# Two attention stages and a gated feed-forward layer: in batches 3 and 4 all six groups of stage 1 share one maximum and one sum

## The chip, the cores and the metric

The kernel runs on one NeuronCore of one Trainium2 chip. The metric is the device time of one execution, in microseconds (µs). Before the change three runs gave a median of 714.13 µs (713.99 to 714.23).

The engines are named as the profile names them: PE is TensorE (matrix products; PEld its weight loads), DVE is VectorE, ACT is ScalarE, POOL is GpSimd, and SP is SyncE, which here only starts DMAs. Each engine works through its own list of instructions in order and waits for others by semaphores.

## The reference, cut to what matters

```python
def mab(q, kv):                                   # one attention
    s = scale * (q @ kv.transpose(0, 2, 1))
    s = s - s.max(-1, keepdims=True)
    a = np.exp(s)
    a /= a.sum(-1, keepdims=True) + 1e-09
    return a @ kv
h = mab(I, x)                                     # stage 1: 32 inducing points attend to 12416 tokens
y = mab(x, h)                                     # stage 2: every token attends to the 32 rows of h
gate = 1.0 / (1.0 + np.exp(-(y @ w_gate)))        # feed-forward, 128 -> 1536 -> 128
out = (gate * (y @ w_val)) @ w_out
```

There are 4 batches of 12416 tokens with 128 channels. Stage 1 needs a maximum and a sum over all tokens of a batch, and stage 2 of a batch can only begin when stage 1 of that batch is complete.

## The kernel before

**Tiling.** A batch has 97 columns of 128 tokens: six groups of 16 columns (numbers 0 to 5) and one column left over (number 6, `NG` in the code). Stages 1 and 2 work by groups, the feed-forward by blocks of four columns (512 tokens).

**The main loop.** A block passes through the feed-forward in 8 steps, by turns of two and of one 128-wide slices of the 1536. `product(t)` issues for step t the matmuls that fill `v_ps` (the value half), the fill of the gate half `g_ps` for step t + 2, and the VectorE instruction that multiplies both halves into `u` (L1071). `gate(t + 2)` is ScalarE's tanh (L1053), which reads `g_ps` into `t`. `project` multiplies `u` by the output weights (L1106), and ScalarE copies the finished block out (L1124). For a two-slice step the product `u` of step t is made to wait for the gate fill of step t + 2, which itself waits until tanh of step t has emptied the same PSUM bank. So tanh, gate fill and product follow one another.

**Slots.** Two steps make a slot. All other work is placed by hand: `at(slot, make)` puts an instruction behind the first step of that slot, and `late=True` behind the second. The loop calls these as it passes; nothing is reordered later. With o = 96 the slots counted from o are those in which batch 2 goes through the feed-forward and stage 1 of batch 3 is computed beside it; with o = 192 the same for batches 3 and 4. In the trace slot 0 of these is at about 201 µs (o = 96) and 369 µs (o = 192), and a slot takes about 1.75 µs.

**Stage 1 beside the loop** (`plan_stage1` and `plan_shared`). The scores of one group fill one PSUM bank, tag `m`, of which there is one; all work beside the loop takes it in turn. In batches 3 and 4 there were two ways for a group before the change:

- Groups 2 and 3, each on its own (`plan_stage1`): VectorE takes the maximum straight from PSUM (L248), ScalarE the exponential from PSUM (L261), the tile is transposed by DMA, the sums are accumulated and copied out by ScalarE (`s1_sum_keep`, L311).
- Groups 0, 1, 4 and 5 together (`plan_shared`): ScalarE copies the scores to SBUF (`keep`, L358), into parts of the transposed input `xT` that nobody reads any more. GpSimd raises one common maximum elementwise, one group after the other (`lift`, three instructions L375, L376 and L379), halves it to 128 columns and joins the left-over column. VectorE reduces those 128 columns (`low`, L389). GpSimd subtracts the maximum from the scores (`lower`, L403), ScalarE takes the exponentials (`weigh`, L407), and pairs of groups share one accumulation in PSUM (`PER` = 2), each copied out once (`hold`, L421).

`plan_combine` then weighs the partial results (two own and two shared, `NSH` = 4) by their maxima and adds them on GpSimd (`least`, `join`).

**Stage 2 beside the loop** (`plan_stage2`). ScalarE copies scores to SBUF (`keep`, L636), GpSimd subtracts each token's maximum (`s2_lower_pool`, L646 to L653), ScalarE takes the exponential (L662), GpSimd adds up (`total`, L670), inverts (L453 to L458) and multiplies (`spread`, L692, tile `a2n`), and a DMA transposes the result for the main loop. GpSimd does the work of both stages in the order of the slots.

Of the kernel before, what the change touches and what calls it, by code (L numbers as in the profile page):

```python
# [9 lines left out]
F32 = mybir.dt.float32  # L10
F16 = mybir.dt.float16
# [6 lines left out]
P = 128  # L18
GC = 16
# [7 lines left out]
def kernel(  # L27
# [10 lines left out]
    B, N, C = x.shape  # L38
    m = inducing.shape[0]
# [4 lines left out]
    NG = NCH // GC  # L44
    NLO = NCH - NG * GC
# [12 lines left out]
    s2p = ctx.enter_context(tc.tile_pool(name="s2p", bufs=2))  # L58
    up = ctx.enter_context(tc.tile_pool(name="up", bufs=6))
    tp = ctx.enter_context(tc.tile_pool(name="tp", bufs=4))  # L60
    op = ctx.enter_context(tc.tile_pool(name="op", bufs=3))

# [114 lines left out]
    arrival = [0, NG] + list(range(1, NG))  # L179
    at_col = {s: p for p, s in enumerate(arrival)}  # L180
    EARLY = NS - 3
    SHARED = [(), (0, 1)] + [(0, 1, 4, 5)] * (B - 2)
    own = [[s for s in (arrival if b == 0 else [2, 3, 4, 5]) if s not in SHARED[b]] for b in range(B)]
    col_of = [{s: p for p, s in enumerate(o)} for o in own]
    PER = [1, 1] + [2] * (B - 2)
    NSH = [len(own[b]) + len(SHARED[b]) // PER[b] for b in range(B)]
    nml = const.tile([P, 1 + NS - EARLY], F32, tag="nml")
    l1l = const.tile([P, 1 + NS - EARLY], F32, tag="l1l")
# [24 lines left out]
    def at(slot, make, late=False):  # L213
        plan.setdefault((slot, late), []).append(make)
# [130 lines left out]
    def plan_shared(b, o, takes, tops, least, weighs, sums, holds, one, with_one):  # L345
        st = {}
        nm, hst, ns, no = nm1s[b % 2], hsts[b % 2], NSH[b], len(own[b])
        per = PER[b]

        def place(i):  # L350
            c = NLO + 8 * i
            return xT[b - 1][:, c : c + 8, :].rearrange("p j t -> p (j t)").bitcast(F32)

        def score(i):
            st["s1"] = s1_score_pe(b, SHARED[b][i], "m")

        def keep(i):
            nc.scalar.copy(out=place(i), in_=st["s1"][:])  # L358

        def score_one():  # L360
            s1 = s1_score_pe(b, NG, "m")
            st["one"] = s1p.tile([P, 512], F16, tag="a1T", name="one").bitcast(F32)[0:m, 0:P]
            nc.scalar.copy(out=st["one"], in_=s1[0:m, 0:P])

        def weigh_one():
            st["a1T"] = s1p.tile([P, 512], F16, tag="a1T", name="a1T")
            nc.scalar.activation(out=st["a1T"][0:m, 0:P], in_=st["one"], func=AF.Exp)

        def turn_one():
            st["a1"] = s1p.tile([P, 4, P], F16, tag="a1", name="a1")  # L370
            nc.sync.dma_start(st["a1"][:, 0, 0:m], st["a1T"][0:m, 0:P], transpose=True)

        def rise(near, far, w, R=P):
            top, r = place(4)[0:R, 0:w], place(5)[0:R, 0:w]
            nc.gpsimd.tensor_tensor(out=r, in0=far, in1=near, op=ALU.subtract)  # L375
            nc.gpsimd.tensor_scalar(  # L376
                out=r, in0=r, scalar1=BIG, scalar2=0.0, op0=ALU.min, op1=ALU.max
            )
            nc.gpsimd.tensor_tensor(out=top, in0=near, in1=r, op=ALU.add)  # L379

        def lift(i):
            rise(place(0) if i == 1 else place(4), place(i), 512)
            if i == len(SHARED[b]) - 1:
                for w in (256, 128):
                    rise(place(4)[:, 0:w], place(4)[:, w : 2 * w], w)
                rise(place(4)[0:m, 0:P], st["one"], P, m)

        def low():
            nc.vector.tensor_reduce(  # L389
                out=nm[:, no : no + 1],  # L390
                in_=place(4)[:, 0:128],
                axis=AX.X,
                op=ALU.max,
                negate=True,
            )
            lower(place(0), st["one"], place(1))
            for k in range(no + 1, ns):
                nc.gpsimd.tensor_copy(out=nm[:, k : k + 1], in_=nm[:, no : no + 1])

        def lower(*parts):  # L400
            for far in parts:
                near = nm[0 : far.shape[0], no : no + 1].to_broadcast(far.shape)
                nc.gpsimd.tensor_tensor(out=far, in0=far, in1=near, op=ALU.add)  # L403

        def weigh(i):
            st["a1T"] = s1p.tile([P, 512], F16, tag="a1T", name="a1T")
            nc.scalar.activation(out=st["a1T"][:], in_=place(i), func=AF.Exp)  # L407

        def turn(i):
            st[i] = s1_turn_dma(b, SHARED[b][i], st["a1T"])  # L410

        def part(i, k0, k1):
            if i % per == 0 and k0 == 0:
                st["hp"] = ps.tile([P, C + 1], F32, tag="m", name="hp_ps")
            if i == with_one and k0:
                s1_sum_pe(b, NG, st["a1"], st["hp"], 0, 1, False, False)
            s1_sum_pe(b, SHARED[b][i], st[i], st["hp"], k0, k1, i % per == 0, (i + 1) % per == 0)

        def hold(k):
            summed[b] += 1  # L420
            nc.scalar.copy(out=hst[:, no + k, :], in_=st["hp"][:])  # L421

        for i in range(len(SHARED[b])):
            at(o + takes[i], lambda i=i: score(i))
            at(o + takes[i], lambda i=i: keep(i), late=True)
            at(o + weighs[i], lambda i=i: weigh(i), late=True)
            at(o + weighs[i] + 1, lambda i=i: turn(i))
            at(o + sums[i], lambda i=i: part(i, 0, 2))
            at(o + sums[i] + 1, lambda i=i: part(i, 2, 4))
        at(o + one[0], score_one)  # L430
        at(o + one[1], weigh_one)
        at(o + one[1] + 1, turn_one)
        for i, slot in enumerate(tops):
            at(o + slot, lambda i=i: lift(i + 1))
        at(o + least, low)
        if len(SHARED[b]) > 2:
            at(o + least + 6, lambda: lower(*[place(i) for i in range(2, len(SHARED[b]))]))
        for k, slot in enumerate(holds):
            at(o + slot, lambda k=k: hold(k))
# [68 lines left out]
    def plan_combine(b, lead, weights, joined, taken, fill):  # L508
# [5 lines left out]
        def least():  # L514
            ml = bp.tile([P, 1], F32, tag="ml")
            src = nm1[:, 0:1]
            for k in range(1, ns, 2):
                nc.gpsimd.tensor_scalar(
                    out=ml[:],
                    in0=src,  # L520
                    scalar1=nm1[:, k : k + 1],
                    scalar2=nm1[:, min(k + 1, ns - 1) : min(k + 1, ns - 1) + 1],
                    op0=ALU.min,
                    op1=ALU.min,
                )
                src = ml[:]
            st["col"] = join_min(bp, ml)

        def weigh():
            st["w"] = bp.tile([P, NS], F32, tag="w1", name="w1")  # L530
# [65 lines left out]


    a2 = {}

    def s2_score(b, c, j0, j1, s2, whole=False):  # L600
        for j in range(j0, j1):
# [109 lines left out]
    def plan_stage2(b, c, score, take, weigh, far=None, soon=False, lag=None, low=None):  # L711
# [58 lines left out]
        if soon:  # L770
            for k in range(2):
                at(weigh - 1 + k, lambda k=k: s2_shift(GC, st["s2"], *st["hl"], which=(k,)))
        else:
            at(take, keep, late=True)
            at(low or take if lag is None else lag, lower, late=lag is None)
        at(weigh, exp, late=True)
        at(weigh + 1, total)
# [279 lines left out]
    def product(t):  # L1057
        st = steps[t]
        hidden_mm(st, "v")
        if t == 0:  # L1060
            keep_on(3, "acc")
        if t < T0:
            gate_fill(t + 2)
        else:
            single_fill(2 * (t - T0) + 3)
            single_fill(2 * (t - T0) + 4)
            st["t"] = ring_t(2 * (t - T0), 2)
        st["u"] = up.tile([P, st["cnt"], 512], F16, tag=f"u{st['cnt']}", name="u16")
        cuts = [0, 256, 512] if t == 0 else [0, 512] if t < NST - 1 else [0, 384, 512]
        for c, e in zip(cuts, cuts[1:]):  # L1070
            u = nc.vector.scalar_tensor_tensor(  # L1071
                out=st["u"][:, :, c:e],
                in0=st["t"][:, :, c:e],
                scalar=1.0,
                in1=st["v"][:, :, c:e],
                op0=ALU.add,
                op1=ALU.mult,
            )
            if t == 0 and c == 0:
                turn_b()  # L1080
        if st["cnt"] == 2 and 4 <= t < T0:

            tc.declare_no_dep(u.ins, st["tanh"].ins, reason="the gate fill of t + 2 waits for it")
            tc.add_manual_dep(
                u.ins, gates[t + 2]["gend"].ins.name, AFTER, reason="tanh, gate fill, product"
            )
# [46 lines left out]
    for b in range(B):  # L1133
# [30 lines left out]
            turns = (5, 7, 17, 19, 22, 25, 9)  # L1164
            shared = (10, 14), (15,), 20, (26, 30), (33, 42), (34, 43), (13, 25), 0
        else:
            parts = {2: (7, (16, 17, 17)), 3: (11, (18, 19, 19))}
            turns = (-14, -5, -3, 2, 0, 8)
            shared = (
                (-6, 2, 10, 14),  # L1170
                (7, 11, 15),
                23,
                (26, 30, 42, 46),
                (40, 42, 49, 51),
                (45, 53),
                (9, 27),
                3,
            )
        plan_shared(b + 1, o, *shared)
        for s, (score, total) in parts.items():  # L1180
# [90 lines left out]
```

## Time and profile before

| | before |
|---|---|
| time, median of 3 runs | 714.13 µs |
| span of the profiled execution, first to last instruction | 712.4 µs |
| around the span (difference of the two) | 1.7 µs |
| PE, ACT busy in the span | 649.5 µs (91%), 678.6 µs (95%) |
| POOL busy in the span | 449.2 µs (63%) |
| granted TensorE clock | 0.998 of full speed |

The profiled execution has no time of its own beside its span; the 1.7 µs come from the median of the runs. Busy time is the time in which an engine has an instruction under way. Successive instructions of one engine overlap a little in the records, so the step from one start to the next is shorter than a recorded duration. In a row of the timeline stand the start in µs, the time that the row covers, engine, line, operation, `output<-inputs`, shapes and the number of instructions merged into it; in square brackets the engine's idle time before it and what ended it.

### The profile page before, as it was taken

What the parts mean: (1) busy time and instruction counts of PE and PEld (TensorE: products, weight loads), DVE (VectorE), ACT (ScalarE), POOL (GpSimd) and SP (SyncE); (2) the same over time, 40 slices, a digit from 0 to 9 for tenths busy, and PEclk for the clock granted to TensorE, in tenths of its full rate; (3) what the DMA queues carried; (4) which work ended last, traced back from release to release, by engine and by line L of the source; (5) the groups of instructions that cost most, each with busy time, mean ns of one, the idle gap of its engine ahead of it and who ended that gap; (6) DMA issues with size and microseconds to landing.
All of it is one profiled execution on the core that took longest, in us unless ns stands there. A gap on an engine that the chain in (4) does not pass through costs nothing.

```text
span 712.4 us, 21620 instructions
## 1 busy us (share of the span) xinstructions
PE 649.5 (91%) x8475; PEld 394.2 (55%) x8475; DVE 694.2 (97%) x806; ACT 678.6 (95%) x1103; POOL 449.2 (63%) x785
## 2 busy tenths in 40 slices
PE   7999899998999999999998989999899999899996
PEld 4555455555555555655555655555555555555555
DVE  4799999999999999999999999999999999999997
ACT  4799999999999999999999999999999999999996
POOL 4568865877558978668657887587748356372300
PEclk9999999999999999999999999999999999999999
DMA  8979964263693174155485142221222131221201
GB/s 171 176 136 174 149 129 103 76 120 81 118 159 81 57 126 103 56 120 114 92 149 112 53 76 67 55 76 38 70 76 61 46 60 60 61 61 46 71 37 46
DMA packets 117110, 65.23 MB, mean 92 GB/s; under 512 B 100208, under 2 KB 101392, under 8 KB 117008
## 3 DMA queue, kind: packets, MB, share of 16 engines
q1 hardware_dynamic: 112320, 49.83, 31.4%
q0 software_dynamic: 4416, 13.90, 11.1%
q8 instruction: 66, 1.08, 0.6%
q14 instruction: 36, 0.29, 0.1%
q10 hardware_dynamic: 272, 0.13, 0.1%
HBM read 27.80 MB, written 25.43 MB: 75 GB/s over the span
## 4 chain that ended last, share of the span: by engine, by line
DVE 38%; PE 30%; issue 15%; ACT 14%; DMA 2%; DVEq 1%; POOL 0%; ACTq 0%; POOLq 0%
DVE u L1071 36%; PE acc_ps L1106 14%; PE v_ps L1022 11%; ACT t L1053 11%; PE g_ps L1022 2%; DMA xn<-in_x_dram 2%; ACT o L1124 2%; ACT xn L1045 1%; PE hp_ps L296 1%; DVE nm L248 1%; DVEq L1071 0%; POOL xn L95 0%; ACT a1T L261 0%; ACT e L662 0%; ACT hwt L483 0%
## 5 line engine op out<-in xcount | busy, mean ns | idle before, releaser
L1071 DVE SCALAR_TENSOR_TENSOR u<-t,v_ps 128x512 f16<-128x512 f16 x609 | 528.8, 947 | 1.0 <-ACT t L1053 0.5
L1053 ACT ACTIVATE t<-g_ps 128x512 f16<-128x512 f32 x609 | 464.5, 821 | 11.0 <-ACT t L1053 4.3
L1106 PE MATMUL acc_ps<-wo,u 128*128 128x128 f16 x4656 | 334.5, 220 | 3.2 <-ACT o L1124 0.8
L1106 PEld LDWEIGHTS <-u 128*128 128x128 f16 x4656 | 262.7, 98 | 112.9 <-issue 109.4
L1022 PE MATMUL v_ps<-a2r,hwt 32*128 32x512 f16 (+1 forms) x1188 | 278.6, 372 | 47.1 <-DVE u L1071 43.5
L1022 PE MATMUL g_ps<-a2r,hwt 32*128 32x512 f16 (+1 forms) x1188 | 293.6, 376 | 0.5 <-DVE u L1071 0.2
L1022 PEld LDWEIGHTS <-hwt 32*128 32x128 f16 x2424 | 92.0, 91 | 156.7 <-issue 104.3
L1071 DVE SCALAR_TENSOR_TENSOR u<-xn,v_ps 128x1024 f16<-128x1024 f16 (+1 forms) x127 | 142.9, 1206 | 0.3 <-PE g_ps L1022 0.3
L1045 ACT ACTIVATE xn<-g_ps 128x512 f16<-128x512 f32 x249 | 129.0, 606 | 1.9 <-PE g_ps L1022 0.6
L692 POOL TENSOR_TENSOR a2n<-e,rs 128x2048 f16<-128x2048 f16 (+3 forms) x25 | 86.8, 3475 | 5.0 <-DVE rs L681 2.1
L670 POOL TENSOR_TENSOR sum<-e 128x256 f32<-128x256 f16 (+1 forms) x23 | 15.4, 672 | 117.0 <-ACT e L662 117.0
L453 POOL TENSOR_TENSOR near<-sme,minus 128x16 f32<-128x16 f32 (+1 forms) x22 | 65.2, 2964 | 1.6
L1124 ACT ACTIVATE o<-acc_ps 128x512 f32<-128x512 f32 x96 | 58.0, 604 | 0.0
L647 POOL TENSOR_SCALAR rise<-rise 128x256 f32<-128x256 f32 (+6 forms) x110 | 30.3, 275 | 9.6
L650 POOL TENSOR_TENSOR top<-top,rise 128x128 f32<-128x128 f32 (+3 forms) x88 | 28.5, 323 | 7.3
L670 POOL TENSOR_TENSOR sum<-sum 128x128 f32<-128x128 f32 (+3 forms) x92 | 28.4, 309 | 7.2
L646 POOL TENSOR_TENSOR rise<-top 128x128 f32<-128x128 f32 (+3 forms) x88 | 27.3, 311 | 6.9
L646 POOL TENSOR_TENSOR rise<-sc 128x256 f32<-128x256 f32 (+1 forms) x18 | 13.3, 736 | 21.2 <-ACT sc L636 21.1
L653 POOL TENSOR_TENSOR sc<-sc,top 128x512 f32<-128x512 f32 (+1 forms) x18 | 19.5, 1086 | 1.4
L602 PEld LDWEIGHTS <-xT 128*128 128x128 f16 x388 | 13.1, 96 | 11.7 <-issue 11.3
L95 POOL DMA_DIRECT2D xn<-in_x_dram x25 | 15.0, 607 | 6.5 <-DMA xn<-in_x_dram 5.6
L602 PE MATMUL s_ps<-hT,xT 128*128 128x32 f16 x388 | 18.1, 178 | 0.1
(161 smaller groups left out, 321.7 us busy)
## 6 DMA issues: line engine op xcount, KB each, us to landing
out_dram<-o SPq DMA_DIRECT2D x96, 256.0 KB, 2.1
xn<-in_x_dram POOLq DMA_DIRECT2D x19, 512.0 KB, 7.2
xn<-in_x_dram POOLq DMA_DIRECT2D x4, 544.0 KB, 6.0
a2r<-a2n SPq DMA_TRANSPOSE x29, 4.4
xT<-xn SPq DMA_TRANSPOSE x27, 4.4
xn<-in_x_dram POOLq DMA_DIRECT2D x1, 384.0 KB, 14.9
wg<-in_moe_w_gate_dram POOLq DMA_DIRECT2D x1, 384.0 KB, 16.4
wv<-in_moe_w_val_dram POOLq DMA_DIRECT2D x1, 384.0 KB, 16.4
```

Of the source, the lines that this page charges most:

```text
L453: nc.gpsimd.tensor_tensor(out=near, in0=x, in1=minus, op=ALU.pow)
L602: nc.tensor.matmul(s2[:, j, :], xT[b][:, c + j, :], hT16[b][:], start=(j == 0), stop=whole and j == j1 - 1, skip_group_check=True,)
L646: nc.gpsimd.tensor_tensor(out=r, in0=far, in1=near, op=ALU.subtract)
L647: nc.gpsimd.tensor_scalar(out=r, in0=r, scalar1=BIG, scalar2=0.0, op0=ALU.min, op1=ALU.max)
L670: nc.gpsimd.tensor_tensor(out=d[:, 0:n, :], in0=src[:, :, 0:w], in1=src[:, :, w : 2 * w], op=ALU.add)
L692: eng.tensor_tensor(out=a2n[:, 0:n, :, :], in0=e.unsqueeze(2).to_broadcast((P, n, 4, m)), in1=rs.unsqueeze(2).unsqueeze(3).to_broadcast((P ...
L1022: st[what + "end"] = nc.tensor.matmul(pt[:, k, col : col + nb * P], hw[b][r : r + 32, j // 2, :], a2r[r : r + 32, o : o + nb, :].rearrange ...
L1045: nc.scalar.activation(out=ring_t(i, 1), in_=singles[i]["g"][:], func=AF.Tanh, scale=0.5)
L1053: st["tanh"] = nc.scalar.activation(out=st["t"][:, :, c:e], in_=st["g"][:, :, c:e], func=AF.Tanh, scale=0.5)
L1071: u = nc.vector.scalar_tensor_tensor(out=st["u"][:, :, c:e], in0=st["t"][:, :, c:e], scalar=1.0, in1=st["v"][:, :, c:e], op0=ALU.add, op1= ...
L1106: nc.tensor.matmul(acc[0][:, i, :], st["u"][:, n, ts(i, P)], wo16[:, NI * (e % 2) + e // 2, :], start=(e == 0 and i == 0), stop=(e == NJ - 1),
L1124: nc.scalar.mul(out=o32[:], in_=acc[0][:], mul=0.5)
```

## The change

In batches 3 and 4 all six groups now go the shared way, and the timetable of stage 1 is dealt anew:

- `SHARED` lists all six groups for these batches and `PER` is 6: one maximum, one accumulation over six groups in the bank `m`, one `hold`. `plan_stage1` isn't called for them (`parts` is empty), so L248, L261 and L311 fall away there, and `NSH` is 1.
- Scores of the fifth and sixth group in the list go to two new SBUF tiles `far`. To make room, the output ring `op` has 2 buffers in place of 3, and the ring of one-slice products `u1` has 5 in place of 6.
- The running maximum and its scratch move to other parts of `xT` (`top_at`, `rise_at`), since those of before now hold scores.
- GpSimd raises the maximum five times in place of three, at slots 3, 8, 11, 12 and 15 in place of 7, 11 and 15. `least` (the point where VectorE reduces) stays at slot 23, the first exponential at slot 26.
- Two copies of scores are issued half a slot sooner: the stage 1 copy at slot 10, and the stage 2 copy at slot 6.

```diff
-    op = ctx.enter_context(tc.tile_pool(name="op", bufs=3))
+    op = ctx.enter_context(tc.tile_pool(name="op", bufs=2))
...
-    SHARED = [(), (0, 1)] + [(0, 1, 4, 5)] * (B - 2)
+    SHARED = [(), (0, 1)] + [(0, 1, 2, 4, 3, 5)] * (B - 2)
...
-    PER = [1, 1] + [2] * (B - 2)
+    PER = [1, 1] + [6] * (B - 2)
...
+        homes = (0, 1, 2, 3, 4, 5) if len(own[b]) else (0, 1, 4, 5, "a", "b", 2, 3)
+        top_at, rise_at = (4, 5) if len(own[b]) else (6, 7)
...
         def place(i):
-            c = NLO + 8 * i
+            if homes[i] in ("a", "b"):
+                return spare[homes[i]][:]
+            c = NLO + 8 * homes[i]
             return xT[b - 1][:, c : c + 8, :].rearrange("p j t -> p (j t)").bitcast(F32)
...
         def score(i):
+            if homes[i] in ("a", "b"):
+                spare[homes[i]] = s1p.tile([P, 512], F32, tag="far" + homes[i], name="far", bufs=1)
             st["s1"] = s1_score_pe(b, SHARED[b][i], "m")
...
         def lift(i):
-            rise(place(0) if i == 1 else place(4), place(i), 512)
+            rise(place(0) if i == 1 else place(top_at), place(i), 512)
...
-            at(o + takes[i], lambda i=i: keep(i), late=True)
+            at(o + takes[i], lambda i=i: keep(i), late=len(own[b]) > 0 or takes[i] not in [10])
...
-            st["col"] = join_min(bp, ml)
+            st["col"] = join_min(bp, src)
...
+    eager = [first_slot + k for first_slot in (NG * GC, 2 * NG * GC) for k in [6]]
...
-            at(take, keep, late=True)
+            at(take, keep, late=take not in eager)
...
-        st["u"] = up.tile([P, st["cnt"], 512], F16, tag=f"u{st['cnt']}", name="u16")
+        st["u"] = up.tile(
+            [P, st["cnt"], 512], F16, tag=f"u{st['cnt']}", name="u16", bufs=4 + st["cnt"]
+        )
...
-            parts = {2: (7, (16, 17, 17)), 3: (11, (18, 19, 19))}
+            parts = {}
...
-                (-6, 2, 10, 14),
-                (7, 11, 15),
+                (-6, 2, 7, 10, 11, 14),
+                (3, 8, 11, 12, 15),
                 23,
-                (26, 30, 42, 46),
+                (26, 30, 35, 39, 42, 46),
-                (40, 42, 49, 51),
-                (45, 53),
-                (9, 27),
-                3,
+                (40, 42, 44, 46, 48, 50),
+                (53,),
+                (9, 43),
+                5,
```

The rows below are the instructions in the order in which they stand on an engine.

The first place is on GpSimd, at slots 1 to 7 of o = 96: `a2n` is the spread of a stage 2 group of batch 2, `rise<-sc` the start of the next group's lowering. Before:

```order
L455 TENSOR_SCALAR rs<-rs 128x16
L458 TENSOR_TENSOR rs<-near,rs 128x16
L692 TENSOR_TENSOR a2n<-e,rs 128x2048
L646 TENSOR_TENSOR rise<-sc 128x256
L647 TENSOR_SCALAR rise<-rise 128x256
```

and with the change:

```order
L467 TENSOR_TENSOR rs<-near,rs 128x16
L702 TENSOR_TENSOR a2n<-e,rs 128x2048
L384 TENSOR_TENSOR xT_880<-xT_880 128x512
L385 TENSOR_SCALAR xT_880<-xT_880 128x512
L388 TENSOR_TENSOR xT_880<-xT_880 128x512
L656 TENSOR_TENSOR rise<-sc 128x256
```

The first lift of the maximum (three instructions) has moved up, between the spread and the lowering.

The second place is GpSimd's list before the shared maximum is halved (`128x256`), at slots 15 to 18. Before:

```order
L379 TENSOR_TENSOR xT_880<-xT_880 128x512
L375 TENSOR_TENSOR xT_880<-xT_880 128x512
L376 TENSOR_SCALAR xT_880<-xT_880 128x512
L379 TENSOR_TENSOR xT_880<-xT_880 128x512
L375 TENSOR_TENSOR xT_880<-xT_880 128x256
```

and with the change:

```order
L388 TENSOR_TENSOR xT_880<-xT_880 128x512
L384 TENSOR_TENSOR xT_880<-far,xT_880 128x512
L385 TENSOR_SCALAR xT_880<-xT_880 128x512
L388 TENSOR_TENSOR xT_880<-xT_880 128x512
L384 TENSOR_TENSOR xT_880<-far,xT_880 128x512
L385 TENSOR_SCALAR xT_880<-xT_880 128x512
L388 TENSOR_TENSOR xT_880<-xT_880 128x512
L384 TENSOR_TENSOR xT_880<-xT_880 128x256
```

Between the lowering of the stage 2 group and the halving there are now four lifts, two of them reading `far`; before there were three. With the one that moved up, that makes five.

The third place is ScalarE's list at slots 25 to 28: `t` are the tanh of the main loop, `a1T<-xT` is the first exponential of stage 1 (`weigh`), `a1T<-one` that of the left-over column. Before:

```order
L1053 ACTIVATE t_5484<-g_ps 128x1024
L1053 ACTIVATE t_5494<-g_ps 128x512
L407 ACTIVATE a1T<-xT_880 128x512
L1053 ACTIVATE t_5518<-g_ps 128x1024
L367 ACTIVATE a1T<-one 32x128
L1053 ACTIVATE t_5530<-g_ps 128x512
```

and with the change:

```order
L1063 ACTIVATE t_5415<-g_ps 128x1024
L1063 ACTIVATE t_5425<-g_ps 128x512
L416 ACTIVATE a1T<-xT_880 128x512
L1063 ACTIVATE t_5449<-g_ps 128x1024
L1063 ACTIVATE t_5459<-g_ps 128x512
L1063 ACTIVATE t_5481<-g_ps 128x1024
```

The first exponential keeps its place among the tanh; that of the left-over column has moved to slot 43.

More of the change, by code (lines that the diff above doesn't have):

```diff
@@ L348, in plan_shared @@
         per = PER[b]
+        homes = (0, 1, 2, 3, 4, 5) if len(own[b]) else (0, 1, 4, 5, "a", "b", 2, 3)
+        top_at, rise_at = (4, 5) if len(own[b]) else (6, 7)
         def place(i):
-            c = NLO + 8 * i
+            if homes[i] in ("a", "b"):
+                return spare[homes[i]][:]
+            c = NLO + 8 * homes[i]
             return xT[b - 1][:, c : c + 8, :].rearrange("p j t -> p (j t)").bitcast(F32)
+        spare = {}
         def score(i):
+            if homes[i] in ("a", "b"):
+                spare[homes[i]] = s1p.tile([P, 512], F32, tag="far" + homes[i], name="far", bufs=1)
             st["s1"] = s1_score_pe(b, SHARED[b][i], "m")
@@ L373, in rise @@
         def rise(near, far, w, R=P):
-            top, r = place(4)[0:R, 0:w], place(5)[0:R, 0:w]
+            top, r = place(top_at)[0:R, 0:w], place(rise_at)[0:R, 0:w]
             nc.gpsimd.tensor_tensor(out=r, in0=far, in1=near, op=ALU.subtract)
@@ L381, in lift @@
         def lift(i):
-            rise(place(0) if i == 1 else place(4), place(i), 512)
+            rise(place(0) if i == 1 else place(top_at), place(i), 512)
             if i == len(SHARED[b]) - 1:
                 for w in (256, 128):
-                    rise(place(4)[:, 0:w], place(4)[:, w : 2 * w], w)
-                rise(place(4)[0:m, 0:P], st["one"], P, m)
+                    rise(place(top_at)[:, 0:w], place(top_at)[:, w : 2 * w], w)
+                rise(place(top_at)[0:m, 0:P], st["one"], P, m)
         def low():
@@ L390, in low @@
                 out=nm[:, no : no + 1],
-                in_=place(4)[:, 0:128],
+                in_=place(top_at)[:, 0:128],
                 axis=AX.X,
```

## The prediction

> **What bounds the kernel.** I read the page first: busy shares, then the chain that ended last.
>
> ```profile
> span 712.4 us, 21620 instructions
> PE 649.5 (91%) x8475; PEld 394.2 (55%) x8475; DVE 694.2 (97%) x806; ACT 678.6 (95%) x1103; POOL 449.2 (63%) x785
> DVE 38%; PE 30%; issue 15%; ACT 14%; DMA 2%; DVEq 1%; POOL 0%; ACTq 0%; POOLq 0%
> ```
>
> Shares over the whole span mix stages, so next come busy times in the two stretches that the change rebuilds, stage 1 of batch 3 and of batch 4. Per engine a row has the busy time within the stretch and the number of instructions.
>
> ```profile
> 192.00:288.00 96.00, 88.21 (x1195) 53.38 (x1191) 96.00 (x113) 94.66 (x145) 71.32 (x122) 1.00 0.51 104
> 360.00:456.00 96.00, 88.21 (x1197) 53.51 (x1193) 96.00 (x113) 94.67 (x144) 69.41 (x119) 1.00 0.42 87
> ```
>
> The columns are PE, PEld, DVE, ACT, POOL. VectorE works 96.00 of 96 µs. Work taken from it is time won, as long as nobody makes it wait; a wait that reaches it is never made up. ScalarE has 1.34 µs to spare in 96, GpSimd 24.7 µs. GpSimd thus looks like the place for more work, but totals don't show when its results are due.
>
> **What the change takes from VectorE.** The timeline of VectorE around the two reductions of a batch:
>
> ```profile
> 214.22 0.68 DVE L248 TENSOR_REDUCE nm<-s_ps 128x1 f32<-128x512 f32 x1
> 214.82 7.08 DVE L1071 SCALAR_TENSOR_TENSOR u<-t,v_ps 128x512 f16<-128x512 f16 x8
> 221.81 0.68 DVE L248 TENSOR_REDUCE nm<-s_ps 128x1 f32<-128x512 f32 x1
> 222.41 20.95 DVE L1071 SCALAR_TENSOR_TENSOR u<-t,v_ps 128x512 f16<-128x512 f16 x24
> 243.27 0.28 DVE L389 TENSOR_REDUCE nm<-xT 128x1 f32<-128x128 f32 x1
> ```
>
> From 214.22 to 214.82 and from 221.81 to 222.41 is 0.60 µs each: 1.20 a batch, 2.40 for both, all before slot 12.
>
> **What it puts on GpSimd, and when that is due.** These rows run from the spread before slot 7 to the first `lower`, on which the first exponential waits.
>
> ```profile
> 206.19 3.61 POOL L692 TENSOR_TENSOR a2n<-e,rs 128x2048 f16<-128x2048 f16 x1
> 213.46 0.74 POOL L646 TENSOR_TENSOR rise<-sc 128x256 f32<-128x256 f32 x1 [3.65 <-ACT sc L636]
> 221.11 1.27 POOL L375 TENSOR_TENSOR xT<-xT 128x512 f32<-128x512 f32 x1
> 222.47 0.61 POOL L376 TENSOR_SCALAR xT<-xT 128x512 f32<-128x512 f32 x1
> 223.17 1.27 POOL L379 TENSOR_TENSOR xT<-xT 128x512 f32<-128x512 f32 x1
> 228.69 1.28 POOL L375 TENSOR_TENSOR xT<-xT 128x512 f32<-128x512 f32 x1 [0.86 <-ACT xT L358]
> 232.10 0.73 POOL L375 TENSOR_TENSOR xT<-xT 128x256 f32<-128x256 f32 x1
> 236.98 0.66 POOL L670 TENSOR_TENSOR sum<-e 128x256 f32<-128x256 f16 x1
> 247.10 1.04 POOL L403 TENSOR_TENSOR xT<-xT,nm 128x512 f32<-128x512 f32 x1
> ```
>
> From 206.19 to 247.10 is 40.91 µs, of which GpSimd waits 3.65 + 0.86 = 4.51; the rest stands back to back. A lift takes 228.69 to 232.10, 3.41 µs. The change puts two more lifts into this stretch, 6.82 µs, and lets lifts fill both waits, as their scores lie ready by then (the last is copied at slot 14, and the fifth lift starts near 231). So the stretch becomes 40.91 - 4.51 + 6.82 = 43.22 µs, and the lowered scores come **2.31 µs later**. VectorE's reduction at slot 23 keeps its cover: the maximum is ready at 236.98 + 2.31 = 239.3. It would cost if that came after 242.1, where VectorE will reach its reduction (243.27 - 1.20).
>
> The two far lifts read tiles of their own, which no row shows. Their bounds are the two-input rows of this size on GpSimd, 1.27 above and, in the next fence, 1.039 (L403). If the two far subtractions took 1.04, the delay would be 0.46 less, 1.85. I take 1.27: it is the same operation on two full operands.
>
> ```profile
> L375 POOL TENSOR_TENSOR xT<-xT 128x512 f32<-128x512 f32 x7 | 8.9, 1272 | 3.6 <-ACT xT L358 3.5
> L403 POOL TENSOR_TENSOR xT<-xT,nm 128x512 f32<-128x512 f32 x10 | 10.3, 1039 | 0.1
> ```
>
> The Trainium skill (GPSIMD Engine Reference, "3.1 Elementwise — side-by-side cycle accounting") gives about 2.6 cycles an element for two inputs and 1.03 for one. At its 1.2 GHz that makes a lift of about 2.66 µs, an estimate from that page, 0.50 less than the three rows here add up to (3.15). Five such lifts would take away the whole delay of 2.31, and its section "4.1 Engine selection" would have kept the maximum on VectorE anyway. Seven lifts in this trace stand at 1272 ns a subtraction, so the measurement decides.
>
> **Who waits for it.** ScalarE's rows at that place, then those of PE and VectorE behind them:
>
> ```profile
> 248.95 0.63 ACT L407 ACTIVATE a1T<-xT 128x512 f16<-128x512 f32 x1
> 249.47 1.03 ACT L1053 ACTIVATE t<-g_ps 128x1024 f16<-128x1024 f32 x1
> 250.55 0.39 PE L1022 MATMUL g_ps<-a2r,hwt 32*128 32x512 f16 x2
> 250.98 1.22 DVE L1071 SCALAR_TENSOR_TENSOR u<-t,v_ps 128x1024 f16<-128x1024 f16 x1
> ```
>
> The scores were lowered at 247.10 + 1.04 = 248.14, and ScalarE came for them at 248.95: a margin of 0.81. With the change they are ready at 250.45, and since the main loop is 1.20 sooner, ScalarE comes at 247.75. It waits 2.7 µs, and behind this exponential stands the tanh of the main loop. The next three rows have no slack: tanh ends at 250.50, the gate fill that waits for it at 250.94, and the product that must wait for the fill starts at 250.98. So the product starts not at 249.78 (250.98 - 1.20), but 2.31 - 0.81 = 1.50, plus some 0.05 to wake ScalarE (tanh's end to the fill's start takes as much), later than before: 252.5. **The 1.20 µs are used up, and 1.55 µs are lost on top.** Behind that point VectorE has as much to do as before and is full, so the loss stays.
>
> Batch 4 shows the same numbers:
>
> ```profile
> 374.06 3.61 POOL L692 TENSOR_TENSOR a2n<-e,rs 128x2048 f16<-128x2048 f16 x1
> 381.32 0.73 POOL L646 TENSOR_TENSOR rise<-sc 128x256 f32<-128x256 f32 x1 [3.65 <-ACT sc L636]
> 396.56 1.27 POOL L375 TENSOR_TENSOR xT<-xT 128x512 f32<-128x512 f32 x1 [0.87 <-ACT xT L358]
> 414.97 1.04 POOL L403 TENSOR_TENSOR xT<-xT,nm 128x512 f32<-128x512 f32 x1
> 416.82 0.63 ACT L407 ACTIVATE a1T<-xT 128x512 f16<-128x512 f32 x1
> ```
>
> From 374.06 to 414.97 is 40.91 again, with 4.52 of waits, and the margin is 416.82 - 416.01 = 0.81. Another 1.55.
>
> **ScalarE's own balance.** A batch gains two copies, reads two exponentials from SBUF in place of PSUM, and copies one result out in place of four:
>
> ```profile
> L261 ACT ACTIVATE a1T<-s_ps,nm 128x512 f16<-128x512 f32 x11 | 7.6, 687 | 2.7 <-DVE nm L248 1.8
> L407 ACT ACTIVATE a1T<-xT 128x512 f16<-128x512 f32 x10 | 6.3, 635 | 0.0
> L358 ACT COPY xT<-s_ps 128x512 f32<-128x512 f32 x10 | 5.9, 592 | 0.0
> L311 ACT COPY hst<-hp_ps 128x129 f32<-128x129 f32 x8 | 2.3, 293 | 0.0
> L421 ACT COPY hst<-hp_ps 128x129 f32<-128x129 f32 x6 | 1.7, 286 | 0.0
> ```
>
> 2 x 0.592 - 2 x (0.687 - 0.635) - 2 x 0.293 - 0.286 = +0.21 µs. That is little, but two exponentials move from slots 7 and 11, where the wait swallows any delay, to slots 35 and 39 behind it: 2 x 0.635 = 1.27 more between slots 28 and 50, 38 µs, in which ScalarE has 38 x 1.34/96 = 0.53 free. Between nothing and 0.74 a batch may reach VectorE. I take 0.2, nearer the lower end, since starts follow each other closer than recorded durations.
>
> **At no cost, each with its cover.** GpSimd's two further `lower` (2 x 1.04) come after the wait; it then rests 3.05 before the next `sum`, and ScalarE's delay adds 1.5 to that rest, against 2.31 + 2.08 of new load: just covered, 0.16 left. The stage 2 transposes behind the spread start 2.31 later and land 4.4 after that, near 254; the gate fills need them from slot 31, three slots of 1.75 behind the product at 250.98 (slot 28), so at 256 in this trace. The sixth exponential (slot 46) is transposed at slot 47 and read at slot 50: 5.2 µs against a landing of 3.2; if it came late, PE would wait with the products behind it. The output ring of two is reused every second block, 2 x 7 µs against 2.1. The `u1` ring of five holds five slots, 8.7 µs, of products, which `project` reads within two slots. The combine gets shorter and isn't waited for. Score copies that make PE wait at slots 7, 10 and 11 delay what GpSimd's 43.22 µs hold up anyway.
>
> ```profile
> 263.53 0.66 POOL L670 TENSOR_TENSOR sum<-e 128x256 f32<-128x256 f16 x1 [3.05 <-ACT e L662]
> out_dram<-o SPq DMA_DIRECT2D x96, 256.0 KB, 2.1
> a2r<-a2n SPq DMA_TRANSPOSE x29, 4.4
> a<-a1T SPq DMA_TRANSPOSE x21, 3.2
> ```
>
> **Sum:** 2 x (1.55 + 0.2) = 3.5 µs on the span of 712.4: 715.9. With the 1.7 around it, that is 714.13 + 3.5 = **717.6**.
>
> **Rivals.**
> *The saving stays (faster).* If GpSimd delivers by the time ScalarE comes, 2.40 are won: 711.7. That decides at 43.22 - 2.31 + 0.81 - 1.20 = 40.52 µs for the stretch, 2.70 less than I sum, 0.54 on each of the five lifts. For it speaks only that far lifts aren't in the trace; 0.46 for both is the most that the rows allow. Chance 0.08. (The figure of the GPSIMD Engine Reference, § 3.1, would give this case; seven lifts speak against it.)
> *The wait is absorbed (no change).* If tanh ran further ahead of the product than the 0.04 that I read there, ScalarE could wait while VectorE works on: 714.1 to 715.5. Against it stands the chain of three rows above. Chance 0.07.
> *ScalarE doesn't recover (slower still).* With its lead gone, it might pay the full 0.74 a batch, and a second late delivery (the 0.16 above) could add as much: 2 x (1.55 + 1.5) = 6.1, 720.2. Against it, the later deliveries have slots to spare. Chance 0.07.
> That the change doesn't do what it says is no rival: VectorE's list shrinks from 806 to 802 instructions.
>
> **How the numbers follow.** My forecast has 0.78. Its low end: far lifts at 1.04 and no pinch, 2 x 1.09 = 2.2, with 0.5 of it absorbed: 715.8. Its high end: 2 x (1.55 + 0.74) = 4.6, and 0.2 for small waits: 718.9. Range 715.8 to 718.9. A difference of 0.2% (1.4 µs) is about what a measurement of this kernel can tell from none. Faster 0.08; same 0.07; slower 0.78 + 0.07 = 0.85.
>
> **What would show it.** In the profile after, VectorE should have two idle times of 2 to 3 µs, some 50 µs behind slot 0, before the product at slot 28, and ScalarE should wait there for GpSimd's `lower`, about 2.7 µs each. GpSimd should show no rest between the spread and that `lower`, 43.2 µs. I am wrong if a lift takes under 2.9 µs, if ScalarE's first exponential finds its scores ready, or if VectorE is idle elsewhere. The four reductions must be gone.

## The result and the profile after

| | before | after |
|---|---|---|
| time, median of 6 runs | 714.15 µs (713.94 to 716.75) | 721.12 µs (719.92 to 722.0) |
| ratio to before, 95% interval | | 1.0095 (1.0084 to 1.0106) |
| profiled execution, its span | 712.4 µs | 718.6 µs (its time 720.5) |

The kernel became 7.0 µs slower; 3.5 had been forecast, and the time lies above the range of 715.8 to 718.9. One execution of all those below, the profiled one of the first experiment, took 1229 µs with its matmuls slow from start to end, and is left out of medians and ratios. From the page of the changed kernel:

```profile
span 718.6 us, 21330 instructions
PE 655.9 (91%) x8475; PEld 395.9 (55%) x8475; DVE 693.5 (97%) x802; ACT 679.7 (95%) x1101; POOL 460.4 (64%) x791
PEclk9999999999999999999999989999999999999999
```

VectorE has its 802 instructions, four fewer, and the totals hardly differ from those of before. The loss shows only at its place. First GpSimd's timeline from the spread to the first `lower`:

```profile
205.91 3.61 POOL L702 TENSOR_TENSOR a2n<-e,rs 128x2048 f16<-128x2048 f16 x1
209.48 1.28 POOL L384 TENSOR_TENSOR xT<-xT 128x512 f32<-128x512 f32 x1
...
230.61 1.27 POOL L384 TENSOR_TENSOR xT<-far,xT 128x512 f32<-128x512 f32 x1
...
238.90 0.66 POOL L680 TENSOR_TENSOR sum<-e 128x256 f32<-128x256 f16 x1
...
249.02 1.04 POOL L412 TENSOR_TENSOR xT<-xT,nm 128x512 f32<-128x512 f32 x1
```

No row in that stretch has an idle time in brackets any more. It is 249.02 - 205.91 = 43.11 µs long, forecast were 43.22, and a far lift's subtraction takes 1.27 like any other. Next ScalarE, TensorE and VectorE behind it (three timelines; in the brackets the idle time before the row and what ended it):

```profile
246.55 1.51 ACT L1063 ACTIVATE t<-g_ps 128x1024 f16<-128x1024 f32 x2
250.09 0.63 ACT L416 ACTIVATE a1T<-xT 128x512 f16<-128x512 f32 x1 [2.03 <-POOL xT L412]
250.63 2.56 ACT L1063 ACTIVATE t<-g_ps 128x1024 f16<-128x1024 f32 x3
```

```profile
249.52 0.39 PE L1032 MATMUL v_ps<-a2r,hwt 32*128 32x512 f16 x2
251.69 0.39 PE L1032 MATMUL g_ps<-a2r,hwt 32*128 32x512 f16 x2 [1.78 <-ACT t L1063]
...
252.55 1.46 PE L1118 MATMUL acc_ps<-wo,u 128*128 128x128 f16 x12
253.94 0.61 PE L1032 MATMUL v_ps<-a2r,hwt 32*128 32x512 f16 x2
```

```profile
252.12 1.82 DVE L1083 SCALAR_TENSOR_TENSOR u<-t,v_ps 128x1024 f16<-128x1024 f16 x2 [2.05 <-PE v_ps L1032]
254.60 30.69 DVE L1083 SCALAR_TENSOR_TENSOR u<-t,v_ps 128x1024 f16<-128x1024 f16 x34 [0.67 <-PE g_ps L1032]
```

The wait came where the prediction put it: ScalarE waits for `lower`, tanh is late, the gate fill is late, and the product at slot 28 starts at 252.12 in place of 250.98. This trace ran 0.28 ahead of the other at slot 0, so it is 1.42 later; forecast were 1.55. But then something follows that was not forecast. The twelve matmuls at 252.55 take 1.46 µs where the same twelve take 0.84 elsewhere, and VectorE waits a second time, 0.67. Batch 4 has more of it:

```profile
423.40 1.82 DVE L1083 SCALAR_TENSOR_TENSOR u<-t,v_ps 128x1024 f16<-128x1024 f16 x2 [2.12 <-PE v_ps L1032]
425.92 1.82 DVE L1083 SCALAR_TENSOR_TENSOR u<-t,v_ps 128x1024 f16<-128x1024 f16 x2 [0.71 <-PE g_ps L1032]
428.28 1.82 DVE L1083 SCALAR_TENSOR_TENSOR u<-t,v_ps 128x1024 f16<-128x1024 f16 x2 [0.54 <-PE g_ps L1032]
430.39 25.00 DVE L1083 SCALAR_TENSOR_TENSOR u<-t,v_ps 128x1024 f16<-128x1024 f16 x28 [0.29 <-PE g_ps L1032]
```

The granted clock in these stretches, from busy times by window (the columns are PE, PEld, DVE, ACT, POOL, then the clock, the DMA share and GB/s):

```profile
245.00:252.30 7.30, 5.02 (x56) 2.72 (x55) 5.25 (x7) 5.08 (x9) 7.05 (x8) 1.00 0.42 95
252.40:255.70 3.30, 3.30 (x27) 2.15 (x27) 2.63 (x3) 2.92 (x5) 2.72 (x8) 0.50 0.39 86
255.80:260.00 4.20, 3.80 (x46) 2.17 (x44) 4.10 (x7) 3.79 (x6) 3.60 (x10) 1.00 0.14 48
416.00:423.00 7.00, 4.71 (x55) 2.79 (x55) 5.28 (x7) 4.86 (x8) 6.80 (x7) 1.00 0.35 85
423.10:429.80 6.70, 6.70 (x52) 3.94 (x48) 5.15 (x6) 5.29 (x9) 5.45 (x16) 0.50 0.36 88
```

**Right behind each wait TensorE was granted half its clock**, for 3.41 µs in batch 3 and for 6.83 µs in batch 4. In the trace of before the clock is 1.00 in the same windows:

```profile
252.40:255.70 3.30, 2.92 (x36) 1.69 (x32) 3.30 (x5) 3.25 (x6) 2.55 (x10) 1.00 0.24 85
423.10:429.80 6.70, 5.93 (x72) 3.42 (x70) 6.70 (x9) 6.62 (x11) 3.76 (x6) 1.00 0.21 60
```

The page's `PEclk` line shows only the second of the two, as one 8 among the nines (the slice from 413 to 431 µs). A slice is 18 µs long, and 3.4 µs of half the clock still leave 0.9 of it.

### The profile page after: what moved, and what is told of

Same layout as the page of the kernel before. It is cut to its first block, busy times and chain, and to the rows that moved or that the text cites. A ratio compares the mean times of both kernels' runs of the same rounds, so it can differ in the third digit from the quotient of the medians.

```text
span 718.6 us, 21330 instructions
## 1 busy us (share of the span) xinstructions
PE 655.9 (91%) x8475; PEld 395.9 (55%) x8475; DVE 693.5 (97%) x802; ACT 679.7 (95%) x1101; POOL 460.4 (64%) x791
## 3 DMA queue, kind: packets, MB, share of 16 engines
q8 instruction: 66, 1.08, 0.6%
## 5 line engine op out<-in xcount | busy, mean ns | idle before, releaser
L1118 PEld LDWEIGHTS <-u 128*128 128x128 f16 x4656 | 265.5, 98 | 117.9 <-issue 114.2
L388 POOL TENSOR_TENSOR xT<-xT 128x512 f32<-128x512 f32 (+3 forms) x20 | 18.9, 943 | 1.7
```

The source lines that it names most:

```text
L1118: nc.tensor.matmul(acc[0][:, i, :], st["u"][:, n, ts(i, P)], wo16[:, NI * (e % 2) + e // 2, :], start=(e == 0 and i == 0), stop=(e == NJ - 1),
```

## Experiments

Theory A, formed from these two traces, has three parts: ScalarE's wait for GpSimd (1.4 µs a batch net of the saving), TensorE's halved clock as a consequence of its own idleness in that wait, and small waits behind slot 34 because ScalarE has two more exponentials there. The rivals stand in the expectations. "Before" ran beside each group of kernels, with medians of 714.0 to 714.1 µs and single executions up to 717.75.

### The wait taken away: the first exponential two slots later

```diff
-                (26, 30, 35, 39, 42, 46),
+                (28, 30, 35, 39, 42, 46),
```

> The changed kernel with one number different: the first exponential of stage 1 stands at slot 28 in place of 26 (batches 3 and 4). Theory A (the loss is ScalarE's wait for GpSimd's lowered scores and what follows from it): ScalarE reaches the exponential some 3.5 us later, at about 251.2 by the clock of before, when the scores have been ready since 250.1; no wait over 0.2 us on VectorE at slot 28, no slice with a granted clock under 0.9 near 252 or 423 us. The saving of 1.20 us a batch stays; ScalarE's own load behind slot 28 takes 0.7 to 1.4 us a batch of it: 713.4 to 714.7 us. Rival B (the loss comes from another part of the change: the smaller rings, one accumulation held for 13 slots, memory contention): still 718 or more.

Measured: ten executions between 714.44 and 718.8 µs, median 716.59, ratio 1.0032 (1.0017 to 1.0046). That is 4.5 µs of the loss gone, but 713.4 to 714.7 were expected, so the number was missed. For a usable trace the same kernel was profiled once more:

> The kernel with the first exponential at slot 28 once more, for its trace. Theory A: the wait of 2 us before the product at slot 28 is gone; what its time has above 714.4 us stands in the clock rows as stretches of 3.4 us at half the clock, behind a short wait of TensorE; without such a stretch the time is 714.4 to 714.6 us. A rival, that the spread is not the clock, would show the extra time as waits with the clock at 1.0.

Measured: 714.36 µs. VectorE's wait of 2 µs is gone in both batches; the largest one left is 0.40, at slot 30. So the wait for GpSimd carries most of the loss, and rival B falls. But the change's saving isn't there either: 714.4 is no faster than before. And this trace doesn't explain the spread of 4 µs. The clock alone isn't its cause: an execution of 716.15 µs had a mean granted clock of 1.000.

### TensorE kept busy, the wait left in place

```diff
+        if t in (2 * (NG * GC + 28), 2 * (2 * NG * GC + 28)):
+            keep_on(7, "m", wo16[:, 0:4, :])
         if t < T0:
             gate_fill(t + 2)
```

> The changed kernel with seven added matmuls of 512 columns into the free bank m, whose result nobody reads, issued on TensorE between the value half and the gate fill of the product at slot 28, where TensorE otherwise idles 1.7 us waiting for tanh. ScalarE's wait for GpSimd stays. Theory A (TensorE's idling made the chip grant it half its clock for 3.4 and 6.8 us): the granted clock stays at 1.0 behind 252 and 423 us, VectorE's wait at slot 28 stays at about 2.1 us, the waits of 0.75 and 0.18 (batch 3) and 0.79, 0.62 and 0.37 (batch 4) behind it go, 2.7 in all: about 718.4 us. Rival C (the clock drops for another reason, or the small waits have another cause): 720 to 722 as with the change.

Measured: 717.56 µs (five of six between 717.44 and 717.6), ratio 1.0045 (1.0029 to 1.0062). TensorE and VectorE at that place, and the window behind it:

```profile
249.87 1.68 PE L121 MATMUL w_ps<-wo 128*128 128x512 f16 x7
251.58 0.39 PE L1032 MATMUL g_ps<-a2r,hwt 32*128 32x512 f16 x2
```

```profile
252.01 10.47 DVE L1085 SCALAR_TENSOR_TENSOR u<-t,v_ps 128x1024 f16<-128x1024 f16 x12 [1.92 <-PE v_ps L1032]
```

```profile
252.40:255.70 3.30, 2.83 (x37) 1.82 (x36) 3.30 (x5) 3.26 (x6) 2.72 (x8) 1.00 0.61 164
423.10:429.80 6.70, 5.86 (x70) 3.37 (x68) 6.70 (x9) 6.62 (x11) 5.62 (x15) 1.00 0.27 72
```

VectorE waits 1.92 µs, about as with the change (2.05), and not a second time: it works 3.30 of 3.30 and 6.70 of 6.70 µs. The clock stays at 1.00. Useless matmuls in the gap made the kernel 721.12 - 717.56 = **3.6 µs faster**. That is the size of the clock's part, half of the whole loss (718.4 had been expected; the two profiled spans differ by 2.9). It shows that TensorE's idleness brought the clock down. Rival C falls.

### GpSimd made late in the kernel before

```diff
...
-        for i, slot in enumerate(tops):
-            at(o + slot, lambda i=i: lift(i + 1))
+        if b > 1:
+            at(o + 3, lambda: rise(place(0), place(1), 512, to=(2, 3)))
+        for i, slot in zip((1, 2, 2, 3), (8, 11, 12, 15)) if b > 1 else zip((1,), tops):
+            at(o + slot, lambda i=i: lift(i))
```

> The kernel before, with GpSimd made late alone: two lifts more in batches 3 and 4, one that nobody reads at slot 3 and the lift of the third group done twice (a maximum taken twice is the same maximum), at slots 3, 8, 11, 12, 15 as in the change. VectorE keeps all its reductions. Theory A: the lowered scores come 2.1 to 2.3 us later, ScalarE waits about 1.4, the product at slot 28 comes 1.4 us later, in both batches; if TensorE idles long enough for the clock to drop, 0.9 to 1.8 more a batch. 717.0 us without the drop, 719 to 720 with it. Rival D (a late GpSimd is absorbed by ScalarE's lead): 714.2.

Measured: 719.13 to 721.6 µs, median 720.36, ratio 1.0080 (1.0061 to 1.0099). ScalarE, and the windows behind the two waits:

```profile
250.50 0.63 ACT L407 ACTIVATE a1T<-xT 128x512 f16<-128x512 f32 x1 [1.63 <-POOL xT L403]
```

```profile
252.40:255.70 3.30, 3.03 (x23) 1.40 (x20) 2.19 (x3) 2.60 (x5) 2.80 (x7) 0.54 0.48 92
255.80:260.00 4.20, 4.20 (x37) 2.73 (x36) 3.32 (x5) 3.22 (x6) 3.47 (x10) 0.56 0.17 64
423.10:429.80 6.70, 5.13 (x58) 2.81 (x57) 5.53 (x7) 6.62 (x12) 5.62 (x16) 1.00 0.52 119
```

Two more lifts alone, with nothing else of the change, bring the wait (1.63 µs, the product 1.74 later, in both batches) and the halved clock. Rival D falls: the wait isn't absorbed. TensorE idled 1.38 µs in the one wait and 1.40 in the other; the clock was halved behind the first, for 6.83 µs from 252.63 µs, and not behind the second, at 423 µs. So whether, and for how long, the clock drops varies from wait to wait, which fits times that spread over 2.5 µs here and over 2.1 µs with the change.

The traces show what the two waits differ in. The changes of the clock lie on a fixed grid: in the trace of the change the stretches between them last 245.76, 3.41, 167.25, 6.83 and 286.72 µs, which are 72, 1, 49, 2 and 84 windows of 3.413 µs. Below is TensorE's busy time in the windows of this grid around the waits, first with the change, then in this run (the columns are PE, the clock, the DMA share and GB/s):

```profile
248.95:252.36 3.41, 1.54 (x17) 1.00 0.73 130
419.61:423.02 3.41, 1.67 (x19) 1.00 0.52 96
```

```profile
249.22:252.63 3.41, 1.89 (x19) 1.00 0.69 125
419.89:423.30 3.41, 2.35 (x29) 1.00 0.30 59
423.30:426.71 3.41, 2.44 (x27) 1.00 0.76 146
```

The first three windows each hold a whole wait, and the clock was halved right behind each. The wait of 1.40 µs falls across the edge at 423.30, so that TensorE is busy for 2.35 and 2.44 µs in the two windows that share it, and the clock stays. This fits every wait of this kind in the traces here; no run moved a wait against the grid on purpose.

### The smaller rings alone

```diff
-    op = ctx.enter_context(tc.tile_pool(name="op", bufs=3))
+    op = ctx.enter_context(tc.tile_pool(name="op", bufs=2))
...
+            [P, st["cnt"], 512], F16, tag=f"u{st['cnt']}", name="u16", bufs=4 + st["cnt"]
```

> The kernel before with the change's smaller rings alone: two output buffers in place of three, five one-slice products in place of six. Theory A and the prediction: nothing, 714.15 us within 0.3. Rival B (the rings cause the waits of 0.15 us behind slot 34): VectorE shows such waits and the time is 715 or more.

Measured: median 714.09 µs, ratio 1.0003 (0.9991 to 1.0015); three of twelve executions took 716.4 to 716.6, as single ones of the kernel before do. The rings cost nothing, as forecast.

### A slot later still, and a second wait found

```diff
-                (26, 30, 35, 39, 42, 46),
+                (29, 31, 35, 39, 42, 46),
```

> The changed kernel with the first two exponentials of stage 1 at slots 29 and 31 in place of 26 and 30 (batches 3 and 4), a slot later than in the run with 28. Theory A: scores long ready, no wait of ScalarE for GpSimd; VectorE keeps 0.7 to 1.0 us a batch up to slot 28 and gives back 0.5 to 1.0 a batch to ScalarE's load behind it: 713.0 to 714.4 us in executions whose clock stays at 1.0. If the spread of the run with 28 (714.4 to 718.8) came from short waits of TensorE near slots 28 to 31 that this timetable avoids, the spread is gone here; if it came from elsewhere, it stays.

Measured: median 715.8 µs, 714.08 to 717.97, ratio 1.0020 (1.0007 to 1.0034). The time was missed, and the spread stayed, so it came from elsewhere. This time the trace shows it, near slot 50 of batch 3. TensorE's timeline, VectorE's, and the transpose that SP's queue issued (from the view of tile `a`):

```profile
291.12 0.24 PE L296 MATMUL hp_ps<-xn,a 128*32 128x128 f16 x4 [1.71 <-DMA a<-a1T]
```

```profile
291.87 0.69 DVE L1083 SCALAR_TENSOR_TENSOR u<-t,v_ps 128x512 f16<-128x512 f16 x1 [1.19 <-PE g_ps L1032]
```

```profile
L285 SPq DMA_TRANSPOSE a<-a1T x1: 1202/1202/1202, 284.6 to 284.6; - x1
DMA to landing us min/median/max: 6.4/6.4/6.4
```

The sixth group's transpose landed 6.4 µs after its issue, too late for the sum at slot 50, and VectorE lost 1.19 + 0.36 µs. In the trace of the kernel with 28 the same transpose had landed after 3.5. Beside it a load of 512 KB for a later batch, issued at slot 42 (281.9 µs), took 8.5 µs here and 5.8 there.

### The load moved, or the exponential moved

```diff
-                at(o + (24 if b else 28, 33, 42, 60, 61, 68)[g], lambda b=b, g=g: x_load(b + 2, g))
+                at(o + (24 if b else 28, 33, 51, 60, 61, 68)[g], lambda b=b, g=g: x_load(b + 2, g))
```

> The kernel with the exponentials at slots 29 and 31, and the load of 512 KB of the batch after next moved from slot 42 to slot 51 (it is there only while batch 3's stage 1 is computed). Theory E (the spread of the runs with 28 and 29, and TensorE's wait of 1.7 us near 291 us, come from the sixth group's transpose, which shares the DMA engines with that load and then lands after its sum is due at slot 50): the wait and the spread are gone, every time within 0.4 us, median 714.1 to 714.4. Rival (the transpose comes late for another reason): times from 714 to 718 as before, median near 715.8.

Measured: **714.22 µs, eleven executions between 714.09 and 714.33**, ratio 1.0000 (0.9991 to 1.0009). The same view of the transpose:

```profile
L285 SPq DMA_TRANSPOSE a<-a1T x1: 1202/1202/1202, 284.6 to 284.6; - x1
DMA to landing us min/median/max: 2.4/2.4/2.4
```

2.4 µs without the load beside it, against 6.4. In its main point theory E holds: the load beside it makes the transpose late. That they share DMA engines is the likely reason, but no run shows it apart. The other edit, run on the same chip, leaves the load and has 45 in place of 46 in the timetable with 29:

> The kernel with the exponentials at slots 29 and 31, the load left at slot 42, and the sixth exponential at slot 45 in place of 46, so that its transpose is issued a slot (1.75 us) sooner. Theory E: the wait of 1.7 us at slot 50 is covered or nearly so; spread under 1 us, median 714.1 to 714.6. Rival (the sixth transpose isn't what TensorE waits for): median near 715.8.

Measured: median 714.77 µs, but 714.31 to 720.94, ratio 1.0025 (1.0007 to 1.0042). Half a miss: eight of twelve executions are between 714.31 and 715.32, four above 716. In the profiled one the transpose, issued 1.6 µs sooner, took 2.1 longer:

```profile
L285 SPq DMA_TRANSPOSE a<-a1T x1: 1202/1202/1202, 283.1 to 283.1; - x1
DMA to landing us min/median/max: 8.5/8.5/8.5
```

It landed at 291.6, no sooner than the other (291.0). In this trace, in the one above with 29 and in that with 28 the load landed at 290.9, 290.4 and 287.7 µs, and the transpose 0.5 to 0.7 µs behind it. So its end hangs on the load's end, and an earlier issue doesn't help. Why the load takes 5.8 µs in one execution and 8.8 in another stays open.

### ScalarE's two further exponentials left out

In the kernel with TensorE kept busy, and then in that with the load moved, the third and fourth exponentials of batches 3 and 4 are left out, and the second group's are summed in their place:

```diff
-            at(o + weighs[i], lambda i=i: weigh(i), late=True)
-            at(o + weighs[i] + 1, lambda i=i: turn(i))
+            if b > 1 and i in (2, 3):
+                at(o + weighs[i] + 1, lambda i=i: st.update({i: st[1]}))
+            else:
+                at(o + weighs[i], lambda i=i: weigh(i), late=True)
+                at(o + weighs[i] + 1, lambda i=i: turn(i))
```

> The kernel with TensorE kept busy at slot 28, and in batches 3 and 4 the third and fourth exponentials of stage 1 left out (slots 35 and 39, with their two transposes; the second group's are used in their place, so the output is another). Theory A (the waits of 0.1 us at slots 36 to 44 are ScalarE's load: two exponentials more than before behind slot 28): those waits go, 0.96 us in batch 3 and about 0.7 less what it later wins back in batch 4: 716.0 to 716.4 us against 717.56. Rival (they come from the smaller rings or from the accumulation that holds bank m): 717.3 or more.

Measured: 719.55 µs (718.16 to 720.53), ratio 1.0060 (1.0038 to 1.0083): a miss. This kernel has the load at slot 42, and in the profiled execution the sixth transpose landed after 6.4 µs again; TensorE waited for it 1.65 µs, and its clock was halved for 6.8 µs from there. Between slots 34 and 44, however, nothing is lost any more (0.96 µs in batch 3 without this edit). The clean comparison is the second one:

> The kernel with the exponentials at 29 and 31 and the load at slot 51, and in batches 3 and 4 the third and fourth exponentials left out (slots 35 and 39, with their transposes; the second group's are used in their place, so the output is another). Here neither ScalarE's wait for GpSimd nor the late transpose disturbs. Theory A (the waits of 0.1 us at slots 36 to 44 are ScalarE's load): they go, and with them the loss of 0.97 us in batch 3 (slots 34 to 44) and of 0.7 in batch 4, of which 0.3 was won back behind it: 712.6 to 713.2 us against 714.22, no change up to slot 34. Rival (rings or the bank m held for 13 slots): 714.0 or more.

Measured: 713.14 µs (ten of eleven executions up to 713.55, one 715.83), ratio to before 0.9992 (0.9983 to 1.0001), 1.08 µs below the same kernel with all exponentials. Busy times from 262 to 284 µs, first with all exponentials (load moved), then with two left out:

```profile
262.00:284.00 22.00, 21.45 (x348) 13.46 (x348) 21.55 (x25) 21.59 (x35) 19.50 (x37) 1.00 0.72 134
```

```profile
262.00:284.00 22.00, 21.34 (x371) 13.46 (x372) 22.00 (x27) 21.76 (x34) 19.50 (x37) 1.00 0.60 123
```

VectorE works 21.55 of 22 µs with them and 22.00 without. The small rings and the bank held for 13 slots are still there, so the rival falls. The small waits are ScalarE's load; that the two transposes left out with the exponentials have a part in it was not tested.

## Why the prediction was wrong

*VectorE's saving: right in what goes, short in what stays.* The four reductions are gone. But of 1.20 a batch only 0.71 is there before slot 28 (starts of the same products in the kernel with the load moved, slots 0 to 24, both batches). VectorE has four waits of 0.04 to 0.07 µs between slots 7 and 14. Each costs 0.05 to 0.09 more than that, since the overlap with the instruction before it is lost too; that makes the missing 0.5. The prediction saw such waits and let the wait at slot 28 swallow them, which they are with the change. What causes them was not tested.

*GpSimd's delay: right.* 43.11 against 43.22 µs, no rest, far lifts at 1.27.

*ScalarE's wait and the product at slot 28: right.* 1.42 µs later against 1.55, and 1.30 in each batch with TensorE kept busy.

*Nothing beyond the wait's own length: **this step failed.*** "Behind that point VectorE has as much to do as before and is full, so the loss stays" took TensorE's speed behind the wait as given and put what its idleness does to the clock at nothing. TensorE had idled 1.78 and 1.74 µs and was granted half its clock for 3.41 and 6.83 µs, its matmuls no longer kept ahead of VectorE, and 0.67 µs in batch 3 and 0.71 + 0.54 + 0.29 in batch 4 of idle time came on top. The prediction had named the sign for it, VectorE idle elsewhere, but no cause. Filling the gap gave back 3.6 µs and landed at 717.56, within the range. That it lies on the forecast of 717.6 is luck: errors cancel in it, as told below. The Trainium skill (TensorE: Matmul & The Clock Gate, "Part 1: The HAM clock gate (the "warmup" mystery)") describes a clock of half or full that follows a free-running window of 3413 ns; 3.41 and 6.83 are one and two of these, and the grid of the traces agrees. Its rule in "Why this matters for your kernels" warns of idle gaps over about 3 µs; here gaps of 1.38 to 1.78 µs were enough, and the measurement decides.

*ScalarE's balance: right in kind, too small.* Taken were 0.2 µs a batch; in the kernel with TensorE kept busy slots 34 to 44 cost 0.96 in batch 3 and 0.68 in batch 4, the first even above the 0.74 that stood as upper end. Some 0.6 in all was won elsewhere (0.27 before slot 0, 0.36 behind slot 48 of batch 4; causes not tested), and the product at slot 28 cost 0.25 less a batch than forecast. So terms of the sum were wrong both ways and nearly cancel.

*At no cost: one of them was thin.* The sixth exponential's transpose had 5.2 µs against a landing of 3.2. With the change it landed in time (3.6), but once the main loop ran sooner it took up to 8.5 beside the load. Rings, `least` and the other deliveries cost nothing.

*The rivals.* "Doesn't recover" came nearest in time (720.2), but it is not what happened. The parenthesis in the first rival is off by a little: five lifts shorter by 0.49 each are 2.46, short of the 2.70 that this rival needs. The saving could not stay in any case: with the wait, the clock and the late transpose all taken away, 714.22 is left, no change; ScalarE's two exponentials hold 1.08 of it. No kernel that was run here computes the right output and is faster than the kernel before; by these traces, room on ScalarE behind slot 28 would be the first thing that it needs.

## What to carry to other kernels

Before moving work from the bound engine to an idle one, follow the result to the instruction that waits for it, and look at what is queued behind that instruction on its engine: here the tanh of the main loop, in whose chain nothing had slack. Price a new wait not only by its length but by what TensorE does in it: where a wait leaves TensorE idle for a microsecond or two, look at the granted clock in windows of a few microseconds behind it, since coarse slices can average it away. When the executions of a kernel spread over several microseconds, look for a race for time; a transfer in flight beside a bulk load was the culprit here.

## What was not expected of the hardware

- Idle times of 1.38 to 1.78 µs on TensorE, in stretches where it works about 90% of the time, halved its granted clock for 3.41 or 6.83 µs. Others of 1.40 and 1.71 µs, and one of 2.00, did not, so the length alone doesn't decide. The four that did lie whole within one window of the clock's 3.413 µs grid, in which TensorE was busy for 1.54 to 1.89 µs; the three that did not are cut by an edge of the grid, and no window beside them has less than 2.1 µs of work. This is no exact threshold: the first window of a trace at full clock has as little as 1.85 µs of work without a drop behind it. Why one window was halved in one place and two in the others stays open.
- Seven useless matmuls (1.68 µs) in the gap kept the clock at 1.00 and made the kernel 3.6 µs faster.
- The same small transposing DMA landed after 2.4 µs without, and after 3.5 to 8.5 µs beside, a load of 512 KB; in three of these traces it landed 0.5 to 0.7 µs behind the load, and when it was issued 1.6 µs sooner it landed no sooner.
